# Moving every load and store of an attention-decode backward kernel from the SyncE queue to the GpSimd queue

## The chip, the cores and the metric

The kernel runs on one core of one Trainium2 chip. A core has a matrix engine (TensorE, PE in the profile), two element-wise engines (VectorE, DVE, and ScalarE, ACT), a general one (GpSimd, POOL) and SyncE (SP), which here does nothing but issue transfers. Transfers between HBM and the on-chip memory are carried by 16 DMA engines. An engine issues a transfer by an instruction in its own queue; the transfer then runs by itself and tells its end by a semaphore. The metric is the time of one execution on the device in microseconds (us), the median of the runs.

## The reference

The reference computes softmax attention for one query row per head, and its gradients:

```python
def _fwd_reference(q, k, v):
    scale = q.shape[-1] ** -0.5
    scores = jnp.einsum('bhqd,bhkd->bhqk', q, k) * scale
    attn = _softmax(scores, axis=-1)
    return jnp.einsum('bhqk,bhkd->bhqd', attn, v)
def reference(q, k, v, grad_out):
    _out, _vjp = jax.vjp(_fwd_reference, q, k, v)
    return (_out, *_vjp(grad_out))      # O, dq, dK, dV
```

There are 32 heads, one query row each, 8192 keys and 128 columns, all bfloat16. With p the softmax row and ds = p * (dp - sum(p * dp)) * scale, where dp = V grad_out, the four results are O = p V, dq = ds K, dK = ds (outer product) q and dV = p (outer product) grad_out. K and V are 64 MiB each and are read once; dK and dV are 64 MiB each and are written once. Nothing else is large.

## The kernel before

K and V of a head are tiles of 128 partitions x 64 rows x 128 columns, 2 MiB, 16 KB contiguous per partition (`Kt`, three buffers, and `Vt`, two buffers). dK and dV of a head are made in tiles of the same shape (`G_dk` and `G_dv`, two buffers each).

The loop at L293 runs over the heads with one stage of overlap: pass h does the forward part of head h and the dK and dq part of head h - 1. The order of instructions on each engine is the order in which they are written (`manual_schedule`, L93). In one pass:

- `k_blocks` (L150): DVE transposes K of head h in four pieces into `XK`; `k_scores` (L159): PE multiplies them with the query, 64 small matmuls.
- `ds_of` (L265) and `outer(p_, "dk", r)` (L237), r = 0 to 3: DVE makes ds and then a quarter of dK of head h - 1 with each call; `dq_of` (L274) is the product for dq on PE ("wide": four rows of K side by side in one matmul).
- softmax: DVE and PE find the maximum over the partitions, ACT does the exponential (L333), PE the sum, DVE the reciprocal (L341).
- `v_transposes` (L191), `v_scores` (L202), `wide(h, "o", ...)` (L349): PE transposes V, ACT copies it out of PSUM, PE computes dp and O.
- `outer(h, "dv", r)`: DVE makes dV of head h in four quarters.

Transfers, all on SyncE's queue but one: `rows` from q (L83; the half from grad_out is issued by ACT, L84), `load_k` (L72), `load_v` (L78), the stores in `outer` (L254) and the two small results (L291). K of head 0 is loaded in four parts; dK and dV of the first and the last head are stored in two halves; every other transfer is 2 MiB. Before the loop K0, V0, K1 and V1 are issued, and K2 follows in head 0's pass. From then on each pass issues, in this order, the load of K of head h + 2 (once PE is through with the buffer's old K), the store of dK, the load of V of head h + 2 (once PE is through with V of head h) and the store of dV. A queue takes its instructions in order, so a transfer whose condition isn't met holds those behind it. Transfers use eight completion semaphores in turn; a transfer waits until the eighth before it has landed.

GpSimd builds the 128 x 128 identity, `ident`, by `make_identity` (L91): a memset and a select. `ident` is read by DVE's `in_quad` (L100), by the tiles made from it (`lane`, `ident_f`, `diag`, `q_blk`), and by PE's transposes; DVE does `in_quad` ahead of its first K transpose.

Of the kernel before, what the change touches and what calls it, by code (L numbers as in the profile page):

```python
# [23 lines left out]
def kernel(  # L24
# [11 lines left out]
    nc = tc.nc  # L36
# [25 lines left out]
    Kt, Vt, XK, XV, st = {}, {}, {}, {}, {}  # L62

    def rows_of(x, h, c, parts):
        L = NT // parts
        return x[0, h].rearrange("(p n) d -> p n d", p=P)[:, c * L:(c + 1) * L, :]

    def slots(X, c, parts):
        L = NT // parts
        return X[:, c * L:(c + 1) * L, :]  # L70

    def load_k(h):  # L72
        Kt[h] = kpool.tile([P, NT, D], BF16, tag="K", name="Kt")
        parts = NCH if h == 0 else 1
        for c in range(parts):
            nc.sync.dma_start(slots(Kt[h], c, parts), rows_of(k, h, c, parts))

    def load_v(h):  # L78
        Vt[h] = vpool.tile([P, NT, D], BF16, tag="V", name="Vt")
        nc.sync.dma_start(Vt[h][:], rows_of(v, h, 0, 1))  # L80

    rows = consts.tile([H, 2, D], BF16)
    nc.sync.dma_start(rows[:, 0, :], q.rearrange("b h s d -> (b h s) d"))  # L83
    nc.scalar.dma_start(rows[:, 1, :], grad_out.rearrange("b h s d -> (b h s) d"))  # L84
    load_k(0)
    load_v(0)
    load_k(1)
    load_v(1)

    ident = consts.tile([P, P], BF16)  # L90
# [146 lines left out]
    def outer(h, which, r):  # L237
        x = st[h]
        if r == 0:
            x[which] = gpool.tile([P, NT, D], BF16, tag=which, name="G_" + which)  # L240
        G, dst = x[which], out_2 if which == "dk" else out_3
        rep, row = x["ds"] if which == "dk" else x["p"], x["qd"][:, 0 if which == "dk" else 1, :]
        Q = NT // 4
        nc.vector.tensor_tensor(  # L244
            slots(G, r, 4).rearrange("p n (a b) -> p n a b", b=R),
            slots(rep, r, 4).unsqueeze(2).to_broadcast([P, Q, D // R, R]),
            row.rearrange("p (a b) -> p a b", b=R).unsqueeze(1).to_broadcast([P, Q, D // R, R]),
            op=ALU.mult)
        parts = 1
        if h == 0 or h == H - 1:  # L250
            parts = 2
        if r % (4 // parts) == 4 // parts - 1:
            c = r // (4 // parts)
            nc.sync.dma_start(rows_of(dst, h, c, parts), slots(G, c, parts))  # L254

    def rows_bc(h):
        x = st[h]
# [26 lines left out]
    def result(src, dst):  # L284
        half = small.tile([P, H], BF16, tag="half", name="half")
        nc.scalar.copy(half[:], src[:])
        fin_ps = psT.tile([P, CH, P], BF16, tag="T", name="fin_ps")
        nc.tensor.transpose(fin_ps[0:H, 0, :], half[:], ident[:])
        fin_sb = small.tile([H, D], BF16, tag="fin", name="fin_sb")
        nc.scalar.copy(fin_sb[:], fin_ps[0:H, 0, :])  # L290
        nc.sync.dma_start(dst.rearrange("b h s d -> (b h s) d"), fin_sb[:])  # L291

    for h in range(H + 1):  # L293
        p_ = h - 1
# [8 lines left out]
        if h > 0:  # L303
            ds_of(p_)
            outer(p_, "dk", 0)
            dq_of(p_, 0)
# [3 lines left out]
        if h > 0:  # L310
            dq_of(p_, 1)
            outer(p_, "dk", 1)
        if 0 < h and h + 2 < H:
            load_k(h + 2)
# [7 lines left out]
        if h > 0:  # L322
            outer(p_, "dk", 2)
            dq_out(p_)
# [38 lines left out]
        if 0 < h and h + 2 < H:  # L363
            load_v(h + 2)
# [3 lines left out]
        if h == H - 1:  # L368
            result(o_all, out_0)

    result(dq_all, out_1)
    order.__exit__(None, None, None)

# [29 lines left out]
```

## Time and profile before

| | |
|---|---|
| median of three timed runs | 648.25 us (648.2 to 648.41) |
| the profiled execution | 648.14 us, span 646.3 us |
| granted TensorE clock, mean | 0.684 |
| PE / DVE / ACT / POOL busy | 528.0 / 506.1 / 214.5 / 0.7 us |
| moved by DMA | 269.49 MB, mean 417 GB/s |
| transfers of 2 MiB, from issue to landing | 29.3 us (V), 31.1 (K), 34.0 (dV), 33.8 (dK), medians |

How to read it: the page is made from one execution. Busy times are sums over the instructions of an engine; matmuls are pipelined, so PE's number is not its work at full rate. SPq, ACTq and POOLq are the instruction queues in which those engines issue transfers. The landing time of a transfer includes its wait behind other transfers in the queue of the DMA engines. A row of the timeline has the start, the time taken, engine, line, operation and, in brackets, how long the engine was idle before it and what ended that. The chain of waits is followed back from the last instruction; it shows what each step waited for last.

### The profile page before, as it was taken

What the parts mean: (1) busy time and instruction counts of PE and PEld (TensorE: products, weight loads), DVE (VectorE), ACT (ScalarE), POOL (GpSimd) and SP (SyncE); (2) the same over time, 40 slices, a digit from 0 to 9 for tenths busy, and PEclk for the clock granted to TensorE, in tenths of its full rate; (3) what the DMA queues carried; (4) which work ended last, traced back from release to release, by engine and by line L of the source; (5) the groups of instructions that cost most, each with busy time, mean ns of one, the idle gap of its engine ahead of it and who ended that gap; (6) DMA issues with size and microseconds to landing.
All of it is one profiled execution on the core that took longest, in us unless ns stands there. A gap on an engine that the chain in (4) does not pass through costs nothing.

```text
span 646.3 us, 15913 instructions
## 1 busy us (share of the span) xinstructions
PE 528.0 (82%) x7113; PEld 423.2 (65%) x7113; DVE 506.1 (78%) x655; ACT 214.5 (33%) x396; POOL 0.7 (0%) x6
## 2 busy tenths in 40 slices
PE   3988998889899987889877898877897788977781
PEld 3677776766777766667665776656675666766570
DVE  5988888889888778877788777797777977778861
ACT  2334333333343332343313333223432334332340
POOL 0000000000000000000000000000000000000000
PEclk9877665677776656777567765667765777656775
DMA  8999999999999999999999999999999999999984
GB/s 354 399 428 426 425 425 428 424 425 427 427 430 426 429 427 426 429 429 427 429 426 428 428 431 426 427 429 425 429 429 427 427 428 429 427 427 425 423 358 189
DMA packets 19700, 269.49 MB, mean 417 GB/s; under 512 B 2352, under 2 KB 2352, under 8 KB 2864
## 3 DMA queue, kind: packets, MB, share of 16 engines
q1 hardware_dynamic: 19584, 268.47, 98.0%
q8 instruction: 56, 0.92, 0.6%
q14 instruction: 12, 0.10, 0.0%
q10 hardware_dynamic: 48, 0.01, 0.0%
HBM read 134.23 MB, written 134.23 MB: 415 GB/s over the span
## 4 chain that ended last, share of the span: by engine, by line
DMA 49%; DVE 24%; PE 22%; ACT 2%; issue 1%; SPq 0%; ACTq 0%; DVEq 0%
DMA Kt<-in_k_dram 49%; DVE XK_sb L155 15%; DVE G_dv L244 8%; PE w_ps L221 6%; PE s_ps L166 6%; PE T_ps L197 4%; PE dp_ps L234 3%; ACT w_sb L228 1%; ACT p_rep L343 1%; PE s_ps L182 1%; PE m_ps L334 0%; DVE rinv L341 0%; PE dp_ps L209 0%; DVE pdt L268 0%; ACT XT_sb L188 0%
## 5 line engine op out<-in xcount | busy, mean ns | idle before, releaser
L197 PE MATMUL T_ps<-ident_f,Vt 128*128 128x128 f32 x1024 | 202.8, 365 | 1.6 <-ACT XT_sb L188 1.3
L197 PEld LDWEIGHTS T_ps<-ident_f,Vt 128*128 128x128 f32 x1024 | 180.1, 206 | 12.1 <-ACT XT_sb L188 12.1
L244 DVE TENSOR_TENSOR G_dv<-p_rep,qd 128x2048 bf16<-128x2048 bf16 x128 | 148.2, 1220 | 30.5 <-DMA out_dram<-G_dv 27.5
L244 DVE TENSOR_TENSOR G_dk<-ds_rep,qd 128x2048 bf16<-128x2048 bf16 x128 | 155.7, 1218 | 1.1
L155 DVE STREAM_TRANSPOSE XK_sb<-Kt 128x1024 f32<-128x1024 f32 x128 | 148.2, 1213 | 4.9 <-DMA Kt<-in_k_dram 4.6
L188 ACT COPY XT_sb<-T_ps 128x1024 f32<-128x1024 f32 x128 | 128.6, 1008 | 44.5 <-PE T_ps L197 40.8
L166 PE MATMUL s_ps<-q_blk,XK_sb 128*128 128x4 bf16 x2048 | 59.7, 168 | 70.0 <-DVE pdt L268 63.3
L166 PEld LDWEIGHTS <-XK_sb 128*128 128x128 bf16 x2048 | 56.9, 104 | 76.8 <-DVE pdt L268 69.9
L228 ACT COPY w_sb<-w_ps 128x512 f32<-128x512 f32 x64 | 37.6, 587 | 175.5 <-PE w_ps L221 175.4
L209 PEld LDWEIGHTS <-XT_sb 128*128 128x128 bf16 x2048 | 60.7, 98 | 36.9 <-ACT XT_sb L188 23.3
L209 PE MATMUL dp_ps<-do_blk,XT_sb 128*128 128x2 bf16 x2048 | 65.5, 164 | 20.5 <-ACT XT_sb L188 20.5
L234 PEld LDWEIGHTS dp_ps<-diag,w_sb 128*128 128x128 f32 x256 | 56.9, 327 | 17.3 <-ACT w_sb L228 17.3
L221 PE MATMUL w_ps<-Kt,ds_rep 128*32 128x512 bf16 x512 | 67.1, 625 | 0.4 <-DVE ds_rep L270 0.4
L234 PE MATMUL dp_ps<-diag,w_sb 128*128 128x1 f32 x256 | 59.7, 354 | 7.3 <-ACT w_sb L228 7.3
L341 DVE RECIPROCAL rinv<-m_ps 128x1 f32<-128x1 f32 x32 | 5.4, 168 | 70.1 <-PE m_ps L334 70.1
L343 ACT ACTIVATE p_rep<-e,rinv 128x256 bf16<-128x256 f32 x32 | 16.2, 507 | 58.0 <-DVE rinv L341 58.0
L221 PE MATMUL w_ps<-Vt,p_rep 128*32 128x512 bf16 x512 | 34.0, 386 | 0.0
L234 PE MATMUL m_ps<-diag,w_sb 128*128 128x1 f32 x256 | 33.0, 250 | 0.0
L234 PEld LDWEIGHTS m_ps<-diag,w_sb 128*128 128x128 f32 x256 | 31.0, 191 | 0.0
L282 ACT COPY dq_all<-dp_ps 128x1 f32<-128x1 f32 x32 | 5.1, 159 | 62.5 <-PE dp_ps L234 62.5
L321 PEld LDWEIGHTS m_ps<-ident_f,top 128*128 128x128 f32 x32 | 5.8, 182 | 29.0 <-DVE top L319 29.0
L182 PEld LDWEIGHTS s_ps<-sm,lane 128*32 128x32 f32 x256 | 10.4, 151 | 17.5 <-DVE sm L172 16.6
(51 smaller groups left out, 220.9 us busy)
## 6 DMA issues: line engine op xcount, KB each, us to landing
Vt<-in_v_dram SPq DMA_DIRECT2D x32, 2048.0 KB, 29.3
Kt<-in_k_dram SPq DMA_DIRECT2D x31, 2048.0 KB, 31.1
out_dram<-G_dv SPq DMA_DIRECT2D x30, 2048.0 KB, 34.0
out_dram<-G_dk SPq DMA_DIRECT2D x30, 2048.0 KB, 33.8
out_dram<-G_dv SPq DMA_DIRECT2D x4, 1024.0 KB, 15.0
out_dram<-G_dk SPq DMA_DIRECT2D x4, 1024.0 KB, 13.4
Kt<-in_k_dram SPq DMA_DIRECT2D x4, 512.0 KB, 5.2
out_dram<-fin_sb SPq DMA_DIRECT2D x2, 8.0 KB, 12.9
```

The lines of the kernel that those rows point to most:

```text
L155: nc.vector.transpose(XK[h][:, :, :, u, :], slots(Kt[h], u, NCH).rearrange("p g d -> p (g d)").bitcast(F32).rearrange("p (g w j) -> p g w ...
L166: nc.tensor.matmul(out[:, g, :], lhsT=cols[:, g, c // 2, c % 2], rhs=q_blk[:, h, c, :], start=(c == 0), stop=(c == 2 * NB - 1), skip_group ...
L182: nc.tensor.matmul(x["s"][a * QD:(a + 1) * QD, 128:128 + NT], lhsT=lane[:], rhs=x["sm"][:, a].rearrange("p u g -> p (u g)"), start=True, s ...
L188: nc.scalar.copy(X[:], st[h].pop("T")[:])
L197: nc.tensor.transpose(T_ps[:, i, :], words[:, m * P:(m + 1) * P], ident_f[:])
L209: nc.tensor.matmul(st[h]["dp"][:, n:n + 2], lhsT=X[:, i, e2, :], rhs=do_blk[:, h, e2, :], start=(e2 == 0), stop=(e2 == 1), skip_group_chec ...
L221: nc.tensor.matmul(x["w"][a * QD:(a + 1) * QD, :], lhsT=rep[:, n:n + 2 * R, :].rearrange("p n r -> p (n r)"), rhs=Xt[:, 4 * g:4 * g + 4, : ...
L228: nc.scalar.copy(x["wsb"][:].rearrange("p k d -> p (k d)"), x.pop("w")[:])
L234: nc.tensor.matmul(out_col, lhsT=X[:, k, :], rhs=diag[:, k:k + 1], start=(k == 0), stop=(k == R - 1), skip_group_check=True)
L244: nc.vector.tensor_tensor(slots(G, r, 4).rearrange("p n (a b) -> p n a b", b=R), slots(rep, r, 4).unsqueeze(2).to_broadcast([P, Q, D // R, ...
L321: nc.tensor.transpose(x["m"][:, 128:256], top[:].to_broadcast([P, P]), ident_f[:])
L343: nc.scalar.activation(x["p"][:], e[:].unsqueeze(2).to_broadcast([P, NT, R]), ACT.Copy, scale=rinv[:])
```

## The change

Every transfer that `nc.sync` issued is issued by `nc.gpsimd`: loads of q, K and V, stores of dK and dV and the two small results. The load of grad_out stays with ACT. No transfer changes its size, its shape or the data it waits for, and the programs of PE, DVE and ACT are the same instruction by instruction. SyncE is left without transfers. GpSimd's program has the transfers in SyncE's old order, and the identity among the first of them: q, the four parts of K0, V0, K1, V1, then the memset of `ident`, then K2 (which waits for the landing of q, whose semaphore it reuses), then the select of `ident`, then the stores and loads of the loop.

```diff
--- before.py
+++ after.py
@@ -73,14 +73,14 @@
         Kt[h] = kpool.tile([P, NT, D], BF16, tag="K", name="Kt")
         parts = NCH if h == 0 else 1
         for c in range(parts):
-            nc.sync.dma_start(slots(Kt[h], c, parts), rows_of(k, h, c, parts))
+            nc.gpsimd.dma_start(slots(Kt[h], c, parts), rows_of(k, h, c, parts))
 
     def load_v(h):
         Vt[h] = vpool.tile([P, NT, D], BF16, tag="V", name="Vt")
-        nc.sync.dma_start(Vt[h][:], rows_of(v, h, 0, 1))
+        nc.gpsimd.dma_start(Vt[h][:], rows_of(v, h, 0, 1))
 
     rows = consts.tile([H, 2, D], BF16)
-    nc.sync.dma_start(rows[:, 0, :], q.rearrange("b h s d -> (b h s) d"))
+    nc.gpsimd.dma_start(rows[:, 0, :], q.rearrange("b h s d -> (b h s) d"))
     nc.scalar.dma_start(rows[:, 1, :], grad_out.rearrange("b h s d -> (b h s) d"))
     load_k(0)
     load_v(0)
@@ -251,7 +251,7 @@
             parts = 2
         if r % (4 // parts) == 4 // parts - 1:
             c = r // (4 // parts)
-            nc.sync.dma_start(rows_of(dst, h, c, parts), slots(G, c, parts))
+            nc.gpsimd.dma_start(rows_of(dst, h, c, parts), slots(G, c, parts))
 
     def rows_bc(h):
         x = st[h]
@@ -288,7 +288,7 @@
         nc.tensor.transpose(fin_ps[0:H, 0, :], half[:], ident[:])
         fin_sb = small.tile([H, D], BF16, tag="fin", name="fin_sb")
         nc.scalar.copy(fin_sb[:], fin_ps[0:H, 0, :])
-        nc.sync.dma_start(dst.rearrange("b h s d -> (b h s) d"), fin_sb[:])
+        nc.gpsimd.dma_start(dst.rearrange("b h s d -> (b h s) d"), fin_sb[:])
 
     for h in range(H + 1):
         p_ = h - 1
```

## The prediction

> **What bounds the kernel now.** I read the page from the top: the share of each engine, the DMA row of the 40 slices, the table of DMA queues.
>
> ```profile
> span 646.3 us, 15913 instructions
> PE 528.0 (82%) x7113; PEld 423.2 (65%) x7113; DVE 506.1 (78%) x655; ACT 214.5 (33%) x396; POOL 0.7 (0%) x6
> ...
> DMA  8999999999999999999999999999999999999984
> ...
> q1 hardware_dynamic: 19584, 268.47, 98.0%
> ```
>
> No compute engine is above 82%, while the DMA engines are busy in every slice, almost all of it on one queue, the one SyncE issues to. The 268.47 MB are fixed by the problem: K and V in, dK and dV out. So the run is about as long as the DMA engines need for those bytes, plus what they lose at the two ends. GpSimd does six instructions in 0.7 us.
>
> Next the chain of waits in order of time, because a 98% queue can still be fed too late:
>
> ```profile
> 206.99 4.53 DVE XK_sb L155 x4
> 211.58 1.87 PE s_ps L166 x64
> 215.54 30.49 DMA Kt<-in_k_dram
> 246.06 4.62 DVE XK_sb L155 x4
> 250.74 1.87 PE s_ps L166 x64
> 254.69 31.14 DMA Kt<-in_k_dram
> 285.86 4.62 DVE XK_sb L155 x4
> ```
>
> Up to about 215 us the chain runs through DVE and PE: compute is ahead of nothing but itself, and its transposes come every 18.55 us (95.77 to 114.33). Later every second head waits some 31 us for its K, and two heads take 39.8 us (246.06 to 285.86), 19.9 us a head. Compute needs 18.55 us a head, the transfers 19.9: there are 1.35 us a head to spare on the compute side, and a K load stands 30 us in the queue behind others of 4.9 us each (2.10 MB at 427 GB/s, the usual slice). A later issue of such a load is hidden as long as the queue in front of it is not empty.
>
> Then the two ends, in stretches (busy time and count of each engine, granted clock, DMA share, GB/s), and the start in order of time:
>
> ```profile
> 0.00:4.00 4.00, 0.82 (x5) 0.42 (x5) 1.99 (x12) 1.68 (x3) 0.70 (x6) 1.00 0.45 125
> 4.00:8.00 4.00, 0.00 (x0) 0.00 (x0) 3.49 (x7) 0.36 (x2) 0.00 (x0) 1.00 1.06 421
> 8.00:12.00 4.00, 1.73 (x64) 1.73 (x64) 2.20 (x2) 0.00 (x0) 0.00 (x0) 1.00 1.01 433
> 635.00:640.00 5.00, 0.00 (x0) 0.00 (x0) 0.00 (x0) 0.00 (x0) 0.00 (x0) 0.50 0.45 187
> 640.00:646.30 6.30, 0.00 (x0) 0.00 (x0) 0.00 (x0) 0.00 (x0) 0.00 (x0) 0.50 0.04 18
> ```
> ```profile
> 0.73 0.20 POOL masks.py:197 MEMSET ident<- 128x128 bf16 x1 [0.29 <-POOLq L387]
> 0.74 0.39 SPq L83 DMA_DIRECT2D rows<-in_q_dram  x1
> 1.01 0.29 POOL masks.py:199 TENSOR_SCALAR_AFFINE_SELECT ident<-ident 128x128 bf16<-128x128 bf16 x1
> 1.19 1.84 SPq L76 DMA_DIRECT2D Kt<-in_k_dram  x4
> 1.33 0.29 DVE L101 TENSOR_REDUCE in_quad<-ident 128x4 f32<-128x128 bf16 x1 [0.27 <-POOL ident masks.py:199]
> 5.13 5.08 DVE L155 STREAM_TRANSPOSE XK_sb<-Kt 128x1024 f32<-128x1024 f32 x4 [0.43 <-DMA Kt<-in_k_dram]
> 41.52 0.34 SPq L80 DMA_DIRECT2D Vt<-in_v_dram  x1
> ```
>
> Compute ends at 632.6 us with a 0.26 us copy; the last 10 us are drain, at a DMA share of 0.45 and then 0.04. Some of the 16 engines are done and one is not: in the trace's landing events the last 1 MB store reaches its first engine's end at 636.0 us and its last one's at 645.2; for the load of K1, near 18 us, that spread was 2 us. The time is therefore that of the slowest DMA engine, which works without a break from 2.2 us (first packet) to 645.
>
> The profiled execution took 648.14 us, 1.8 around its span of 646.3; the median of the three timed runs is 648.25. My sum starts at 648.2.
>
> **The change part by part.** 138 transfers (1 of q, 35 of K, 32 of V, 34 each of dV and dK, 2 of results) leave the SyncE queue for GpSimd's; bytes, order, waits on PE and DVE, and the program of PE, DVE and ACT are the same. Both queues reuse eight completion semaphores in turn, so a transfer still waits for the eighth before it.
>
> *1. Price of an issue on GpSimd.* No row has one. SyncE takes 0.33 to 0.49 us (0.34 for the V load at 41.52; 1.84 for four K parts); below that I see no gain, since nothing waits on SyncE's issue time. Above, the whole 8 KB load of q takes 1.7 us from issue to landing (1.9 for grad_out): an issue that costs more than a complete small transfer is my upper end, 1.9. It is software on an engine that so far does single small instructions; the two rows are about equally near, so I take the middle, 1.1 us. The Trainium skill's page "DMA: Bandwidth & Descriptors", Specifications, gives a first byte after about 1 us on this path and 0.6 us on SyncE's; by that figure, which no run here shows, the start below would be 0.4 us later and the sum 649.8.
>
> *2. Steady state.* Four issues a head are 4.4 us (7.6 at the upper end) of GpSimd in 19.9 us, and the queue holds some 30 us of work: nothing. Where GpSimd waits for PE to free V (SyncE's longest such wait is 9.6 us), only later transfers stand behind it, as before.
>
> *3. Start of the stream.* SyncE: q at 0.74, first K part at 1.19, first packet at 2.2. GpSimd: q 0.73 to 1.83, first K part to 2.93; the part's packets followed SyncE's issue end (1.65) by 0.57, so they start at 3.5: **+1.3 us** on the path, since the slowest engine never pauses later. Ends: 0 at 0.44 us an issue; at 1.9, +2.9 for two issues and 4 x 0.65 more, because a 0.52 MB part lasts only 1.25 us: +5.
>
> *4. The identity.* It is built on GpSimd, at 0.73 and 1.01. In the new order of GpSimd eight issues stand before its memset (q, four K parts, V0, K1, V1) and a ninth, K2, before its select. 9 x 1.1 = 9.9: ident is ready at 11.1 us, not 1.3. DVE's next instruction, in_quad, waits for it, and behind it stand DVE's small constants (2.7 us of work) and then the K transposes: they start near 14.0 instead of 5.13, but no longer wait for parts (5.08 becomes 4.6): compute of head 0 is **8.4 us late**. Is that hidden? The transfers queued at the start last to 28.4 us on the fastest engine (K2's first landing event) and 31.1 on the slowest; both move 1.3 later. First dV store: issue 19.36 + 8.4 = 27.8, packets 1.7 later at 29.5, against 29.7: in time. The tightest is the V3 load, 41.52 + 8.4 + 1.7 = 51.6: the queue before it empties on the fastest engine at 48.0 + 1.3 = 49.3, on the slowest at 50.7 + 1.3 = 52.0. The fast engines pause, the slowest does not, by 0.4 us. Afterwards compute regains 1.35 us a head. At 0.44 us an issue: 0. At 1.9: ident at 18.3, compute 15.6 late, V3 packets at 59.6 against 50.7 + 5 = 55.7: +4. With a margin of 0.4 us, I put **+1.2** in the sum, a little above the lower end.
>
> *5. Rate of the slowest engine.* If the packets stay 16 KB, as the trace's packet records have them (median 611 ns on one engine), nothing changes. If this queue cuts them smaller: an 8 KB packet of this run took 309 ns, a 4 KB packet 159, so a 16 KB row would take 618 or 636 ns, and 984 rows an engine 6.9 or 24.6 us more. (The stretches agree: 421 GB/s while the first K parts with 4 KB rows flow, 433 after.) Below: the drain could be levelled, 0.45 x 5 + 0.04 x 6.3 = 2.5 us of all engines' work in 11.3 us, so 11.3 - 2.5 = 8.8 at most, and 7.5 with 1.3 us left for the last landing. I take 0: rows of the same lengths are asked for. In this trace, on SyncE's path, there is already an engine that ends 9 us after the first. The same page of the Trainium skill, "Latency and other measured facts", speaks against the zero: engines 7 and 15 are usually slower, by its best guess because the descriptor rings of GpSimd's path share ports with them. It gives no size and no run here shows that part yet; at 1% of the run the sum would be 657 instead of 651.
>
> *6. The end.* The last stores queue behind about 12 us of backlog (the last, issued at 632.3, landed at 645.2); 0.7 us more per issue is hidden by it.
>
> Sum: 648.2 + 1.3 + 1.2 = 650.7, rounded up to **650.8 us**.
>
> **The rivals.**
> (a) *Nothing seen*: issue near SyncE's price, all hidden: 648.2 to 649.2. For it: 30 us of queue; against: the first packet waits for two issues with nothing in front.
> (b) *Smaller packets, or a slower slow engine*: 648.2 + 2.5 + 6.9 = 657.6, with 4 KB packets 675. Queue depth covers none of this. Against: the 16 KB rows are contiguous on both sides.
> (c) *Faster*: the slowest engine catches up. Its place is the drain after 635 us; the price is up to -7.5, so 643 with the start's loss. It decides once levelling is worth more than 2.5 us. For it: half of the engines idle there; against: the same engines carry the same bytes, and the 56 instruction fetches of 16 KB that share them (queue q8) stay.
> (d) *DVE is held up*: descriptor work of 4.4 us a head blocks DVE. Past 1.35 us a head compute becomes the bound: 18.55 + 4.4 = 22.95, 32 x 3.05 = +98: about 746 us. For it: DVE is busy 78% of the span. Against: GpSimd and DVE overlap in this trace only in the first 1.3 us, where nothing is seen to stretch. DVE's large rows are 303.9 us of TENSOR_TENSOR and 148.2 of STREAM_TRANSPOSE; its copies and tensor_scalar are short (0.12 to 0.26 us each). The Trainium skill's page "SBUF — State Buffer", section "Who interferes with whom", says that descriptor generation on GpSimd is shut out by DVE's two-port modes, which copies and tensor_scalar have and tensor_tensor has not; by it little would block.
>
> **How the numbers follow.** A difference under 0.2% (1.3 us) can't be told from none here. Chances: forecast (+1.3 to +6 us) 0.50, (a) 0.19, (b) 0.11, (c) 0.16, (d) 0.04. Slower 0.64 (the forecast, (b), (d), less 0.01 for the lower edge), same 0.20, faster 0.16. The range runs from 644 (the far end of (c) left out) to 668: (b) with 8 KB packets at 657.6, the upper ends of steps 3 and 4 on top (5 + 4 - 2.5 = 6.5, so 664), and a little towards the 4 KB case, which with (d) is left out. The likeliest case alone is 649.5 to 654.
>
> **What would show it.** GpSimd's issue rows near 1.1 us; the first K packet near 3.5; ident near 11 and the first K transpose near 14 us; DVE and PE groups with unchanged means; one software queue with 98% and 19,700 packets; no gap in the GB/s row after the second slice; the chain still ending in a drain behind the stores. Wrong, if the packet count doubles, if TENSOR_TENSOR at L244 rises above 1,220 ns, if GB/s in the middle slices leaves 423 to 431, or if the drain shrinks below 8 us.

## The result and the profile after

The changed kernel takes 649.14 us (median of 20 runs, 648.88 to 650.38), the kernel before 648.24 us in the same runs. The ratio is 1.0015 with a 95% interval of 1.0009 to 1.0022: slower by 0.9 us, a difference that is real but below the 0.2% that the prediction set as the least it would call a change. The profiled execution took 649.20 us, 1.06 more than that of before; its span is 647.4 us, 1.1 more.

From the page of the changed kernel, the span, the share of each engine, the DMA row, the queues and DVE's two largest groups:

```profile
span 647.4 us, 15914 instructions
PE 528.6 (82%) x7113; PEld 423.8 (65%) x7113; DVE 505.5 (78%) x655; ACT 214.4 (33%) x396; POOL 73.9 (11%) x144
...
DMA  8999999999999999999999999999999999999984
...
DMA packets 19652, 269.49 MB, mean 416 GB/s; under 512 B 2256, under 2 KB 2304, under 8 KB 2816
...
q0 software_dynamic: 19536, 268.47, 97.9%
...
L244 DVE TENSOR_TENSOR G_dv<-p_rep,qd 128x2048 bf16<-128x2048 bf16 x128 | 148.2, 1221 | 28.3 <-DMA out_dram<-G_dv 24.7
L244 DVE TENSOR_TENSOR G_dk<-ds_rep,qd 128x2048 bf16<-128x2048 bf16 x128 | 155.7, 1219 | 1.1
```

The same bytes now run on a software queue, in packets of the same size (19,652 against 19,700 in all), and the DMA engines are as busy as before. DVE's two groups take 1221 and 1219 ns, against 1220 and 1218: descriptor work on GpSimd does not hold DVE up. GpSimd is busy for 73.9 us instead of 0.7. In the page's GB/s row the fourth and the seventh slice moved 415 and 418 GB/s (426 and 428 before); all others from the third to the 37th lie between 424 and 430.

The start, in order of time:

```profile
1.28 0.64 POOL L83 DMA_DIRECT2D rows<-in_q_dram  x1 [0.83 <-POOLq L387]
1.92 2.13 POOL L76 DMA_DIRECT2D Kt<-in_k_dram  x4
...
5.60 0.22 POOL masks.py:197 MEMSET ident<- 128x128 bf16 x1
5.74 0.53 POOL L76 DMA_DIRECT2D Kt<-in_k_dram  x1
6.36 0.30 POOL masks.py:199 TENSOR_SCALAR_AFFINE_SELECT ident<-ident 128x128 bf16<-128x128 bf16 x1
6.70 0.28 DVE L101 TENSOR_REDUCE in_quad<-ident 128x4 f32<-128x128 bf16 x1 [5.62 <-POOL ident masks.py:199]
...
9.03 4.61 DVE L155 STREAM_TRANSPOSE XK_sb<-Kt 128x1024 f32<-128x1024 f32 x4
...
23.05 0.56 POOL L254 DMA_DIRECT2D out_dram<-G_dv  x1 [16.38 <-DVE G_dv L244]
```

An issue takes 0.53 us (0.64 for the first). The first one begins only at 1.28 us, where SyncE began at 0.74 and where GpSimd itself did the memset of `ident` at 0.73 before; the trace doesn't show what it does in between. The identity is ready at 6.66 us instead of 1.30, the K transposes begin at 9.03 instead of 5.13, the first store is issued 3.7 us later than before (23.05 against 19.36). The first K packet starts at 3.18 us instead of 2.22. The stretches of the changed kernel at both ends (busy time and count of each engine, granted clock, DMA share, GB/s):

```profile
0.00:4.00 4.00, 0.00 (x0) 0.00 (x0) 0.24 (x2) 1.28 (x1) 2.92 (x9) 1.00 0.20 43
4.00:8.00 4.00, 0.82 (x5) 0.43 (x5) 1.27 (x8) 0.00 (x0) 2.58 (x7) 1.00 0.98 375
...
635.00:640.00 5.00, 0.00 (x0) 0.00 (x0) 0.00 (x0) 0.00 (x0) 0.00 (x0) 0.50 0.70 293
640.00:647.40 7.40, 0.00 (x0) 0.00 (x0) 0.00 (x0) 0.00 (x0) 0.00 (x0) 0.50 0.07 28
```

The first 4 us move 43 GB/s instead of 125. From 635 to 640 us the DMA share is 0.70 instead of 0.45: most engines end later by about the later start, while the slowest does not. The chain of waits is of no help here: with GpSimd issuing, the page follows it along GpSimd's queue and puts 83% of it down to "issue".

The end does not show on the page, since the DRAIN rows, which here close an engine's program, aren't counted as busy. For the kernel's closing line the trace has a row for each queue and operation: count, shortest, median and longest duration in ns, start of the first and of the last. Before, and then after:

```profile
L398 POOLq EVENT_SEMAPHORE  x4: 17/17/17, 645.6 to 646.2; - x4
L398 POOLq DRAIN  x3: 34/78/389, 1.0 to 646.0; - x3
L398 SPq DRAIN  x3: 7/7/7, 645.5 to 645.8; - x3
```
```profile
L398 POOLq EVENT_SEMAPHORE  x4: 17/17/17, 646.7 to 647.2; - x4
L398 POOLq DRAIN  x3: 46/87/13352, 633.3 to 647.1; - x3
L398 SPq DRAIN  x3: 7/7/7, 645.5 to 646.9; - x3
```

SyncE's drain, behind its waits for every landing, comes at 645.5 us in both. But GpSimd now has a drain of its own that starts behind its last issue (633.26 us) and lasts 13.35 us, to 646.61; the first of GpSimd's closing semaphores follows at 646.65 instead of 645.60. The last landing is at 645.2 us before and 645.3 after. So three things are seen in this pair: the packets start 0.96 us later, all the same the last of them lands only 0.1 us later, and GpSimd's drain ends 1.3 us behind that landing and delays the close by 1.05 us.

### The profile page after: what moved, and what is told of

It reads as the page before. It is cut to its first block, busy times and chain, and to the rows that moved or that the text cites. A ratio compares the mean times of both kernels' runs of the same rounds, so it can differ in the third digit from the quotient of the medians.

```text
span 647.4 us, 15914 instructions
## 1 busy us (share of the span) xinstructions
PE 528.6 (82%) x7113; PEld 423.8 (65%) x7113; DVE 505.5 (78%) x655; ACT 214.4 (33%) x396; POOL 73.9 (11%) x144
## 2 busy tenths in 40 slices
DMA packets 19652, 269.49 MB, mean 416 GB/s; under 512 B 2256, under 2 KB 2304, under 8 KB 2816
## 4 chain that ended last, share of the span: by engine, by line
issue 83%; POOL 11%; DVE 3%; PE 1%; POOLq 0%; ACT 0%; DVEq 0%; ACTq 0%
POOL out_dram L254 5%; POOL Kt L76 3%; POOL Vt L80 2%; DVE XK_sb L155 1%; DVE G_dv L244 1%; PE s_ps L166 1%; PE T_ps L197 0%; DVE G_dk L244 0%; POOLq L254 0%; DVE sm L172 0%; DVE q_blk L126 0%; POOL rows L83 0%; DVE four L108 0%; ACT p_rep L343 0%; POOL out_dram L291 0%
## 5 line engine op out<-in xcount | busy, mean ns | idle before, releaser
L244 DVE TENSOR_TENSOR G_dv<-p_rep,qd 128x2048 bf16<-128x2048 bf16 x128 | 148.2, 1221 | 28.3 <-DMA out_dram<-G_dv 24.7
L244 DVE TENSOR_TENSOR G_dk<-ds_rep,qd 128x2048 bf16<-128x2048 bf16 x128 | 155.7, 1219 | 1.1
L209 PE MATMUL dp_ps<-do_blk,XT_sb 128*128 128x2 bf16 x2048 | 65.5, 164 | 20.5 <-ACT XT_sb L188 20.5
L80 POOL DMA_DIRECT2D Vt<-in_v_dram x32 | 17.0, 532 | 247.1 <-PE m_ps L356 247.1
L76 POOL DMA_DIRECT2D Kt<-in_k_dram x35 | 18.6, 533 | 187.6 <-PE w_ps L221 187.6
L254 POOL DMA_DIRECT2D out_dram<-G_dk x34 | 18.1, 532 | 87.0 <-DVE G_dk L244 76.0
## 6 DMA issues: line engine op xcount, KB each, us to landing
out_dram<-G_dk POOLq DMA_DIRECT2D x4, 1024.0 KB, 12.3
```

The source lines that it names most:

```text
L76: nc.gpsimd.dma_start(slots(Kt[h], c, parts), rows_of(k, h, c, parts))
L80: nc.gpsimd.dma_start(Vt[h][:], rows_of(v, h, 0, 1))
L209: nc.tensor.matmul(st[h]["dp"][:, n:n + 2], lhsT=X[:, i, e2, :], rhs=do_blk[:, h, e2, :], start=(e2 == 0), stop=(e2 == 1), skip_group_chec ...
L244: nc.vector.tensor_tensor(slots(G, r, 4).rearrange("p n (a b) -> p n a b", b=R), slots(rep, r, 4).unsqueeze(2).to_broadcast([P, Q, D // R, ...
L254: nc.gpsimd.dma_start(rows_of(dst, h, c, parts), slots(G, c, parts))
```

## The experiments

Each ratio is against the kernel before in the same runs. "Stream" is the time from the first K packet to the last landing and "tail" the time from there to the end of the span, both from the trace's records.

**Which end pays?** Theory END puts the 0.9 us down to GpSimd's drain, theory START to the later first packet. Four kernels put one part of the change back, or make one part alone. `start_sync`:

```diff
-            nc.gpsimd.dma_start(slots(Kt[h], c, parts), rows_of(k, h, c, parts))
+            (nc.sync if h <= 2 else nc.gpsimd).dma_start(slots(Kt[h], c, parts), rows_of(k, h, c, parts))
-        nc.gpsimd.dma_start(Vt[h][:], rows_of(v, h, 0, 1))
+        (nc.sync if h <= 1 else nc.gpsimd).dma_start(Vt[h][:], rows_of(v, h, 0, 1))
-    nc.gpsimd.dma_start(rows[:, 0, :], q.rearrange("b h s d -> (b h s) d"))
+    nc.sync.dma_start(rows[:, 0, :], q.rearrange("b h s d -> (b h s) d"))
```

> The nine transfers ahead of the loop (q, four parts of K0, V0, K1, V1, K2) are issued by SyncE again, everything later by GpSimd. Theory END (the added 0.9 us is GpSimd's drain behind the last landing, and the later start is made up on the way): time stays at 649.1 (+0.14% against before), the drain's end about 1.25 us behind the last landing. Theory START (the stream of packets starts 1.0 us later and that is passed on to the end): 648.2, no difference to before. First packet 2.2 us and ident at 1.3 us under both.

Measured: 647.92 us, ratio 0.9994 (0.9985 to 1.0003).

`start_pool` is the mirror, in the kernel before:

```diff
-            nc.sync.dma_start(slots(Kt[h], c, parts), rows_of(k, h, c, parts))
+            (nc.gpsimd if h <= 2 else nc.sync).dma_start(slots(Kt[h], c, parts), rows_of(k, h, c, parts))
-        nc.sync.dma_start(Vt[h][:], rows_of(v, h, 0, 1))
+        (nc.gpsimd if h <= 1 else nc.sync).dma_start(Vt[h][:], rows_of(v, h, 0, 1))
-    nc.sync.dma_start(rows[:, 0, :], q.rearrange("b h s d -> (b h s) d"))
+    nc.gpsimd.dma_start(rows[:, 0, :], q.rearrange("b h s d -> (b h s) d"))
```

> The kernel before, with only the nine transfers ahead of the loop issued by GpSimd. Theory END: 648.2, as before, although the first packet comes at 3.2 us. Theory START: 649.2, +0.15%. If each carries half: 648.7.

Measured: 649.4 us, 1.0018 (1.0009 to 1.0027).

`end_sync`, in the changed kernel:

```diff
-            nc.gpsimd.dma_start(rows_of(dst, h, c, parts), slots(G, c, parts))
+            (nc.sync if h == H - 1 else nc.gpsimd).dma_start(rows_of(dst, h, c, parts), slots(G, c, parts))
-        nc.gpsimd.dma_start(dst.rearrange("b h s d -> (b h s) d"), fin_sb[:])
+        nc.sync.dma_start(dst.rearrange("b h s d -> (b h s) d"), fin_sb[:])
```

> The changed kernel, with the stores of the last head (dV and dK, two halves each) and both small results issued by SyncE. GpSimd's last transfer is then dK of head 30, which should land several us before the end. Theory END: GpSimd's drain is over before the last landing, time 648.1 to 648.3. Theory START: 649.1, because the first packet still comes at 3.2 us.

Measured: 648.12 us, 0.9994 (0.9985 to 1.0003).

`fin_pool`, in the kernel before:

```diff
-        nc.sync.dma_start(dst.rearrange("b h s d -> (b h s) d"), fin_sb[:])
+        (nc.gpsimd if src is dq_all else nc.sync).dma_start(dst.rearrange("b h s d -> (b h s) d"), fin_sb[:])
```

> The kernel before, with only the very last transfer (the 8 KB of dq) issued by GpSimd. Theory END: one such transfer is enough for the drain, so 649.2 (+0.15%), the drain's end about 1.25 us behind the last landing against SyncE's 0.3. Theory START: 648.2, no difference.

Measured: 648.09 us, 0.9995 (0.9986 to 1.0004). This one missed its aim: on a queue of its own the 8 KB did not wait behind SyncE's stores, landed at 638.4 us, and the drain was over long before the end.

Neither theory survives alone: undoing the start takes the 0.9 us away, and undoing the end takes them away as well. The traces say why. Stream and tail of the runs that bear on it, with some from further down (us, one profiled execution each):

```
                body issued by   first packet   last landing   stream   tail
before          SyncE            2.22           645.2          643.0    1.1
start_pool      SyncE            3.14           646.6          643.4    1.3
fin_pool        SyncE            2.22           645.4          643.2    1.1
end_pool        SyncE            2.22           645.8          643.5    1.3
late_start      SyncE            4.07           648.0          644.0    0.9
after           GpSimd           3.18           645.3          642.1    2.1
start_sync      GpSimd           2.22           644.4          642.2    1.8
end_sync        GpSimd           3.17           645.0          641.8    0.9
mixed           GpSimd           1.74           643.9          642.1    0.9
```

There are three terms, not one: the later start (+0.96), a stream of 641.8 to 642.2 us wherever GpSimd issues the middle of the program, against 643.0 to 644.0 where SyncE does, and a longer tail where GpSimd's transfers are the last to land. Undoing either positive term leaves the negative one against the other, and the sum is near zero. The next two runs test the first and the third term on their own.

**A later start alone.** `late_start`, in the kernel before:

```diff
+    for i in range(4):
+        again = consts.tile([H, D], BF16, name=f"again{i}")
+        nc.sync.dma_start(again[:], q.rearrange("b h s d -> (b h s) d"))
     load_k(0)
```

> The kernel before, with four more 8 KB loads of q on SyncE between q and the first part of K0, at about 0.45 us each. The first K packet comes 1.8 us later, the identity as early as before. If a later start is passed on one to one: 650.0 (+0.28%). If the run makes it up on the way, since compute has 1.35 us a head to spare: 648.2.

Measured: 650.43 us, 1.003 (1.0019 to 1.0042), +2.1 for a first packet that is 1.85 us later (4.07 us). Within the interval a later start is passed on to the end in full (in the profiled execution the last landing came 2.85 us later, as the stream was 1.0 longer besides). What compute has to spare does not help, because the slowest DMA engine has nothing to spare.

**The end alone.** `end_pool`, in the kernel before:

```diff
-            nc.sync.dma_start(rows_of(dst, h, c, parts), slots(G, c, parts))
+            (nc.gpsimd if h == H - 1 else nc.sync).dma_start(rows_of(dst, h, c, parts), slots(G, c, parts))
-        nc.sync.dma_start(dst.rearrange("b h s d -> (b h s) d"), fin_sb[:])
+        nc.gpsimd.dma_start(dst.rearrange("b h s d -> (b h s) d"), fin_sb[:])
```

> The kernel before, with the four stores of the last head and both small results issued by GpSimd, so that a GpSimd transfer lands last. Theory of three terms (later start +0.96 us; the body of transfers 0.9 us shorter from GpSimd's queue; GpSimd's drain +1.0 us behind its last landing): only the drain applies, 649.2 (+0.15%), drain ending 1.0 to 1.3 us behind the last landing. Rival (the drain costs nothing of its own, the differences seen are the body's): 648.2.

Measured: 648.65 us, 1.0005 (0.9996 to 1.0014), between the two, with an interval that reaches to both; the trace decides. The drain ended only 0.29 us behind the last landing, not 1.0 to 1.3. So it has no fixed price. Over the runs it goes with the number of transfers that GpSimd has issued:

```
transfers of GpSimd            1     6     9     40     123    129    132    138
drain behind the landing, us   0.08  0.29  0.41  1.68   0.74   0.99   1.07   1.31
```

The first four are 0.042 to 0.08 us a transfer; the last four lie on a line of nearly the same slope, 0.038, and at 0.042 us a transfer they count afresh from near 106. That is a fit to eight points, made after the fact, so it was put to a test with another count: every store in two halves makes 198 transfers. `halves_sync` is the control, `halves_pool` the same edit in the changed kernel:

```diff
-        parts = 1
-        if h == 0 or h == H - 1:
-            parts = 2
+        parts = 2
```

> The kernel before with every store of dK and dV issued in two halves (198 transfers instead of 138, the same bytes). Control for the next run: 648.2 to 649.5; the halves bring packets of 8 KB instead of 16 KB for the stores (309 ns against half of 611, so 492 rows an engine cost 7 ns more each: +3.4 us at most), so up to 651.7 if the slowest engine pays all of it.

> The changed kernel with every store in two halves: 198 transfers of GpSimd. Theory RING (GpSimd's drain behind its last landing costs 0.042 us for each of its transfers, counted afresh after about 106 of them, which fits 0.08 us at 1 transfer, 0.29 at 6, 0.41 at 9, 1.68 at 40, 0.74 at 123, 0.99 at 129, 1.07 at 132, 1.31 at 138): 198 - 106 = 92 transfers, so the drain ends 3.9 us behind the last landing, and the time is the control's + 0.96 (start) - 0.9 (body) + 3.5 (drain beyond SyncE's 0.3) = the control's + 3.6. Theory FIXED (about 1 us for a long program): the control's + 0.9. Issues on GpSimd, six a head of 0.53 us, stay hidden under both.

Measured: 650.15 us for the control (1.0027, 1.0014 to 1.0039) and 653.86 us (1.0082, 1.0067 to 1.0097): 3.7 us apart where the count said 3.6 and a fixed price 0.9. The closing rows of `halves_pool`:

```profile
L396 POOLq EVENT_SEMAPHORE  x4: 17/17/17, 651.2 to 651.8; - x4
L396 POOLq DRAIN  x3: 46/87/14054, 637.1 to 651.6; - x3
L396 SPq DRAIN  x3: 7/7/7, 647.6 to 651.4; - x3
```

The last landing is at 647.35 us and SyncE is through at 647.6, but GpSimd's drain, begun at 637.06, ends at 651.11: 3.76 us behind the landing, against 3.9 from the count. By the trace the two runs differ by a start 0.95 us later, a stream 0.6 us shorter (644.2 against 644.8) and a tail 3.6 us longer. All transfers but the three of 8 KB have 128 packets here, so a price for each packet would fit as well as one for each transfer. The issues, six a head, kept to 0.53 us and cost nothing that the comparison leaves room for.

**Why is the stream shorter?** In the trace's landing events, four transfers of 2 MB take 19.9 us on the slowest engine, evenly so from 300 to 620 us (`mid_pool` and `mixed` aside); between 80 and 300 us such a step varies in every run, in before from 19.5 to 21.4 us. With SyncE issuing the middle there is in the even stretch one place with steps of 20.5 to 20.7 us, and it comes where one instruction fetch of 8 KB (a packet on queue q14) runs: counted from the first packet, at 478 us in before, fin_pool and end_pool, at 468 in late_start, at 508 in start_pool. With GpSimd issuing, a fetch on the same queue comes at 426 to 455 us instead and the step stays at 19.9 (after, start_sync, end_sync). Other fetches of this size, at about 334, 400, 440, 542 and 575 us, come in the runs of both kinds and go with no such step. To have such a fetch fall away, `mid_pool`, in the kernel before:

```diff
-            nc.sync.dma_start(slots(Kt[h], c, parts), rows_of(k, h, c, parts))
+            (nc.gpsimd if 10 <= h < 20 else nc.sync).dma_start(slots(Kt[h], c, parts), rows_of(k, h, c, parts))
-        nc.sync.dma_start(Vt[h][:], rows_of(v, h, 0, 1))
+        (nc.gpsimd if 10 <= h < 20 else nc.sync).dma_start(Vt[h][:], rows_of(v, h, 0, 1))
-            nc.sync.dma_start(rows_of(dst, h, c, parts), slots(G, c, parts))
+            (nc.gpsimd if 10 <= h < 20 else nc.sync).dma_start(rows_of(dst, h, c, parts), slots(G, c, parts))
```

> The kernel before, with the loads and stores of heads 10 to 19 issued by GpSimd; start and end stay with SyncE. Theory FETCH (of the 0.9 us that the body is shorter, 0.6 are one 8 KB instruction fetch for SyncE's queue, at 478 or 508 us, that meets the slowest DMA engine; SyncE then runs through 44 transfers fewer and that fetch falls behind the end or away): the step of 20.5 us between every fourth landing around 480 to 510 us is gone, 647.6 (-0.1%). Theory PATH (packets from GpSimd's queue as such flow a little faster, in proportion to the third of them that moves): 648.0, and the step is still there.

Measured: 651.38 us, 1.0044 (1.003 to 1.0057): neither. The handover itself spoiled it. While both queues hold work, a 2 MB load of the new queue overtakes stores of the old one; the landing steps that end at 176 us and at 396 us are 25.4 and 23.0 us long, and the stretch from 420 to 440 us moved 406 GB/s where before moved 428. The rest of this program runs too irregularly to look for a step of 0.6 us, so the fetch was not taken away. But other runs move it. With 198 transfers on SyncE's queue, `halves_sync` has two such fetches in the even stretch, at 337 and 550 us, and at both a head takes 20.6 to 20.7 us instead of 19.9; `halves_pool` has none of these steps. In `ident_late4` and `ident_late8` the fetch comes at 480 and 487 us and the step with it. So step and fetch go together in the even stretch wherever SyncE issues the middle; how a packet of 309 ns costs 0.7 us is not seen.

The step is 0.7 of the 0.86 us between before and after. The rest can't be told from scatter: counted from the first packet, K of head 24, the last ahead of the step, lands 0.2 us earlier in after, 0.2 in `start_sync`, 0.5 in `end_sync` and at the same time in `mixed`, but 0.4 and 0.6 us later in `fin_pool` and `end_pool`, whose programs are those of before up to the last head.

**How much cover does head 0 have?** By the working of step 4, put for SyncE's queue, a late identity is hidden up to 8.2 us. `ident_late4` and `ident_late8` delay the identity alone, in the kernel before (range(4), range(8)):

```diff
+    order = tc.manual_schedule()
+    order.__enter__()
+
+    filler = consts.tile([P, 2048], F32)
+    for i in range(4):
+        nc.gpsimd.memset(filler[:], 0.0)
     ident = consts.tile([P, P], BF16)
     make_identity(nc, ident[:])
-
-    order = tc.manual_schedule()
-    order.__enter__()
```

> The kernel before, with four memsets of 1 MB in GpSimd ahead of the identity, some 7 to 9 us in all; SyncE issues as before. Step 4 of the prediction: compute of head 0 comes 4 to 6 us later and the slowest DMA engine has at least 8.2 us in hand at the tightest place (V3 issued at 41.5, packets a microsecond later, the queue before it lasting to 50.7): no difference, 648.2. Rival (a late head 0 is passed on): 652 to 654.

> The same with eight memsets, 14 to 18 us: compute of head 0 is 11 to 15 us late, which is past the 8.2 us in hand. Step 4: the time grows by the measured delay less 8.2, so 651 to 655; with no cover at all 659 to 663; if more cover than reckoned, 648.2.

Measured: 650.11 us, 1.003 (1.002 to 1.004), with the first store 5.4 us later than before; and 657.69 us, 1.0141 (1.0126 to 1.0156), with it 12.8 us later. The last landings came 1.9 and 9.1 us later, so the cover is 3.4 and 3.7 us by these two runs, not 8.2; both times lie between what step 4 and its rival gave. Stretches of `ident_late8` (busy time and count of each engine, clock, DMA share, GB/s):

```profile
24.00:28.00 4.00, 3.06 (x56) 2.70 (x53) 1.10 (x4) 1.50 (x7) 0.00 (x0) 1.00 0.84 356
28.00:32.00 4.00, 4.00 (x20) 3.65 (x19) 2.62 (x4) 2.42 (x3) 0.00 (x0) 1.00 0.03 8
...
48.00:52.00 4.00, 4.00 (x51) 2.83 (x50) 3.73 (x5) 3.57 (x5) 0.00 (x0) 0.77 1.04 311
52.00:56.00 4.00, 3.36 (x70) 3.25 (x66) 4.00 (x4) 1.38 (x3) 0.00 (x0) 1.00 0.93 340
```

The gap between the loads and the first store (28 to 32 us) is as reckoned; the store lands 2.2 us later than before. The second loss is not: from 48 to 56 us the engines are busy and move only 311 to 340 GB/s. The V3 load, the tightest place, landed 10.5 us after its issue (12.3 in `ident_late4`), 7.2 us behind the store ahead of it (8.2 in `ident_late4`). Step 4 looked only at the start of its packets, 1.7 us behind the issue on GpSimd, and left the transfer at its usual 4.9 us. In `ident_late8` V2 and K3 took long as well, 6.7 and 7.2 us behind the transfer ahead of them. Packets of 16 KB from 48 to 52 us took 873 ns on average instead of 611. Why transfers behind a short queue ran slower was not settled.

**Start and end on SyncE, the middle on GpSimd.** `mixed`, in the changed kernel, adds to `start_sync` and `end_sync` that q comes through ACT:

```diff
-    nc.gpsimd.dma_start(rows[:, 0, :], q.rearrange("b h s d -> (b h s) d"))
+    nc.scalar.dma_start(rows[:, 0, :], q.rearrange("b h s d -> (b h s) d"))
```

> Transfers ahead of the loop on SyncE, all between on GpSimd, the last head's stores and both results on SyncE again; the load of q moves to ACT's queue ahead of grad_out, so that K0 is SyncE's first issue. Theory of three terms: start 0.45 us earlier than before, body 0.9 us shorter, no drain at the end: 646.9 (-0.21%), faster than both kernels. Rival (start not passed on, body's gain an accident of these programs): 648.2.

Measured: 646.6 us, 0.9973 (0.9963 to 0.9983): faster than both kernels, and within 0.3 us of the sum of the three terms. Its start and its end:

```profile
0.74 0.41 ACTq L83 DMA_DIRECT2D rows<-in_q_dram  x1
...
0.74 1.80 SPq L76 DMA_DIRECT2D Kt<-in_k_dram  x4
```
```profile
L398 POOLq DRAIN  x3: 40/93/24414, 614.8 to 644.5; - x3
L398 SPq DRAIN  x3: 7/7/7, 643.9 to 644.2; - x3
```

K0 is SyncE's first issue, at 0.74 instead of 1.19 us, and GpSimd's long drain (24.4 us from 614.8) is over at 639.2, before the last landing at 643.9.

## Why the prediction was right, and where it was not

The measured 649.14 us lies in the range, and slower is the side that it leaned to. But the likeliest case's own range began at 649.5, and the change stayed within the 0.2% to which it gave a chance of 0.20. The sum of +2.5 us was 0.9. Of its two terms the start is near and the identity is 0, and two terms that it did not have, +1.0 at the end and -0.9 in the stream, nearly cancel, which is luck. A range from 644 to 668 us would have held the time without that, so it says little for the mechanism. By steps:

*Step 1, the price of an issue.* 1.1 us was taken between 0.44 and 1.9; it is 0.53. The lower row, SyncE's, was the near one. The figure of about 1 us that the Trainium skill's page "DMA: Bandwidth & Descriptors", Specifications, gives for the first byte is not far from the 1.26 us between the first K part's issue and its first packet here (1.03 on SyncE), but the difference to SyncE is 0.2 us, not 0.4.

*Step 2, the steady state.* Right: four issues a head are 2.1 us of GpSimd and cost nothing, nor do six a head in `halves_pool`.

*Step 3, the start.* +1.3 was forecast, +0.96 measured, and `late_start` and `start_pool` show that it is passed on in full, as the step said. But the size is near by luck. Two issues at the real price, 0.64 and 0.56 us, would by the step's own working put the first packet at 2.5 us, +0.3. The rest is that GpSimd's first issue begins at 1.28 us and not at 0.73 (1.25 in `start_pool`), and that the packets follow the issue's end after 0.70 us instead of 0.57. (The step's upper end adds up to 2.9 + 2.6 = 5.5, not 5.)

*Step 4, the identity.* Two errors that met. With the real price of an issue compute is 3.7 us late, 2.7 when the later stream is taken off, which is inside the cover; the +1.2 is 0. But the cover was mis-sized at 8.2 us and is about 3.6. Had an issue cost 1.1 us, compute would have been 7.1 us behind the stream and the step, by an estimate from this cover, 3.5 us instead of 1.2. The term that failed is the time of a load behind a short queue: V3 took 7.2 and 8.2 us behind the store ahead of it in the two runs, where the usual 4.9 was left.

*Step 5, the rate of the slowest engine.* 0 was forecast; the stream is 0.86 us shorter, 0.7 of it in the step near 485 us. Rival (b) fell: the packets stayed at 16 KB with a median of 611 ns. The same page, "Latency and other measured facts", has engines 7 and 15 as usually slower; the trace doesn't number the engines, so this can't be seen here, but the slowest did not fall further back: the last 1 MB store's first and last engine were 9.1 us apart before (635.9 and 645.0; the 645.2 of the prediction is the last small result's landing) and 8.0 after. Rival (c) had the slowest engine catch up, but in the drain after 635 us, where nothing was gained: counted from the first packet, K of the last head already landed 0.86 us earlier than before, and the last transfer no more than that.

*Step 6, the end.* This is the step that failed outright: "0.7 us more per issue is hidden" looked at the issue alone. GpSimd's drain behind the last landing, +1.05 us, was in no step and in no rival. Nothing in the profile before shows it, since GpSimd had no transfers to drain.

Together: +0.96 - 0.86 + 1.0 = +1.1 us of span. The time lies where rival (a) put it, 648.2 to 649.2, but not because nothing happened. Rival (d) fell: L244's two groups rose by 1 ns each, to 1221 and 1219, and DVE's busy time did not rise (505.5 against 506.1 us). Two of the prediction's signs of being wrong were met by the letter, this 1221 against 1,220 and the two slices at 415 and 418 GB/s. Neither says more: the loss in those slices was made up, since K of head 15 landed 0.2 us earlier than before, counted from the first packet.

## What to carry to other kernels

Where the DMA engines are the bound and the slowest of them never pauses, the queue that issues the middle of the program hardly matters (0.9 us of 643 here), while everything at the two ends is paid in full: what stands ahead of the first large transfer, and what the issuing engine does behind the last one. So let the engine with the cheapest issue start and end the stream, put the first large load ahead of the small ones, and look at the rows of the closing line, which the page does not count as busy. Where a late start leaves the queue short, the transfers behind it should not be priced with the time that a full queue gives.

## What the runs showed of the hardware that was not expected

GpSimd's drain behind the landing of its last transfer takes about 0.04 us for each transfer it has issued, 0.08 us after one and 1.68 us after 40; 123 to 138 transfers gave 0.74 to 1.31 us and 198 gave 3.76, as if the count began anew after some 106. With transfers in halves the last of these was forecast within 0.2 us; what happens in the drain is not seen.

One kind of instruction fetch of 8 KB, 309 ns long, goes with a step of 0.6 to 0.7 us on the slowest DMA engine whenever SyncE issues the middle of the program. More transfers on SyncE's queue bring more of these fetches and steps (two in `halves_sync`); with GpSimd issuing there is no such step, and other fetches of the same size go with none.

GpSimd's first issue begins 0.5 us later than SyncE's (1.25 to 1.29 us against 0.74) in every run where a transfer stands first in its program.

Two queues that both hold large transfers share the DMA engines, so a handover from one to the other lets loads overtake stores: `mid_pool` lost 3 us to two handovers, while the handovers of `start_sync`, `end_sync` and `mixed`, at the start and in the drain, cost nothing that could be measured.
